# Moving all v loads to ScalarE's DMA queue, with a new search of every engine's order

**Chip, cores, metric.** One Trainium2 chip, one of its cores. The metric is device time in microseconds (us), the median of several executions.

## The reference

Attention in a window of 32 positions to both sides, for 8 batches of 8 heads of 576 x 64, then a gated linear recurrence over the sequence with two projections:

```python
scores = q @ k.T / sqrt(64);  mask = |i - j| <= 32;  attn = softmax(where(mask, scores, -1e9))
x = (attn @ v) as (batch, seq, 512)
val, gate = split(x @ w_in)                 # 512 -> 2 x 512
h[t] = exp(A_log)[0] * h[t-1] + val[t]
out = (gate * sigmoid(gate) * h) @ w_out    # 8 x 576 x 512, float32
```

## The kernel before

Five engines each work through a fixed order, held as a string with one letter per operation (`x` an exponential, `l` or `L` a load, `O` an output). Another string says which engine takes an operation that several could take. A search offline found both. Each engine runs its own list in order and waits, where it must, for the others. The loads of before are one list on SyncE:

```python
elif kd == "ld" and key[0] in "qk":            # 32 of them, 576 KB each, rows of 2304 bytes
    nc.sync.dma_start(out=..., in_=src[b].rearrange(...)[T])
elif kd == "ld" and key[0] == "v":             # 40 of them, rows of 256 bytes
    _, b, x = key
    lo = 128 * x - 32
    p0, p1 = max(0, -lo), min(128, S - lo)
    nc.sync.dma_start(out=bf("v32", b)[p0:p1, x],
                      in_=v[b, :, lo + p0:lo + p1, :].rearrange("h p d -> p h d"))
...
elif kd == "exp":                              # ScalarE alone, 36 of them, between scores and values
    nc.scalar.activation(bf("pr", *key), bf("sc", *key), AF.Exp, bias=0.0, scale=1.0 / 8.0)
...
elif kd == "mask":                             # where TensorE has not added the mask itself
    m = mask.rearrange("p r q -> p (r q)")
    pr = bf("pr", *key)
    (nc.vector if e == "dve" else nc.gpsimd).tensor_tensor(out=pr, in0=pr, in1=m[...], op=ALU.mult)
...
elif kd == "out":                              # 36 of them, 256 KB each
    nc.sync.dma_start(out=out_flat[r0:r0 + 128, :], in_=bf("o", *key))
...
idle = keep_busy(seq, place, 45.0)             # filler matmuls where TensorE is expected to wait
```

The issue of a transfer may first wait until an earlier transfer has landed. This waiting is done by the engine that issues.

The softmax here doesn't subtract the row's maximum and nothing guards it: scores larger than these inputs give would overflow.

Of the kernel before, what the change touches and what calls it, by code (L numbers as in the profile page):

```python
# [21 lines left out]
    ("pe", "xt"): (0.447, 0.66), ("pe", "pj"): (0.864, 1.07), ("pe", "fin"): (0.864, 1.07),  # L22
    ("act", "ev"): (1.012, 1.18), ("act", "exp"): (0.905, 1.09), ("act", "tanh"): (0.48, 0.63),
    ("act", "fev"): (0.495, 0.65), ("act", "cv"): (0.52, 0.68), ("act", "cw"): (0.52, 0.68),
# [11 lines left out]
ENGINES = ("pe", "act", "dve", "pool", "sp")  # L36
START = {"pe": 0.5, "act": 2.5, "dve": 0.5, "pool": 5.0, "sp": 0.8}
SWITCH, CAP, DLAT, DPRE = 0.095, 190, 1.75, 0.65
SLOTS = {"stg": 5, "q16": 2, "k16": 2, "qT": 3, "kT": 3, "v32": 2, "vE": 2, "vO": 2, "pr": 3,
         "rc": 2, "x16": 2, "xT": 2, "f2k": 16, "th": 3, "si": 3, "fu": 2}  # L40
LETTER = {"L": "ld", "w": "cw", "a": "ar", "k": "ck", "K": "trk", "E": "evk", "q": "cq", "Q": "trq",
          "e": "evq", "v": "cv", "h": "sh", "m": "mask", "S": "sc", "x": "exp", "P": "pv", "r":
          "rc", "n": "norm", "t": "xt", "T": "xe", "V": "pjv", "G": "pjg", "s": "scan", "g": "tanh",
          "u": "silu", "f": "fuse", "F": "fin", "o": "fev", "O": "out"}

SEQ = {
    "pe": "mQmQKSKKmSPSQPSmtmPSPSVtVGQGKGmSGPPmVStVPPGVKtGVVQGVSSFFFKGQFFQFmmSPSPKPPtSSFtKQVPPF"
          "GVSGtmmSVSPPVGSQtGKPPGVVSSGQKFVFSSPGFPPtGVQtKFGPSSGQKVFFGQVSSFtPPFVQtGKGPPSVGKVGVFFS"
          "SVGtFPPSFQtKVQVSSPGVGGFKFPPPFtVSSSGtFVGVGSPFFVFVPPPVFtGGVGVtGFVGGVFFFFFFF",
    "act": "qexExhxexwhwwxwwxgegEgxhvxTgkTEgwgegqxooxEgovooeoxxETxxEoeogxgTxxgxegEkvgvxxgeEooxxg"  # L50
           "kqogveEogxvxEgqooegxokxeogEgvxgvgEoxxogToxoeEexxgkgoEovgvoTxxgxoggooxoTggoTgogggoooo"
           "oo",
    "dve": "akaEehkhrnqrnETrnrnssTussuhvhurrnnshsrsrnnsussssusussvusmmqehvhurnrnrnrnqTmmrnrsnhhu"
           "ussrrnnsumTurrnnsushhmusrmmnrunrnTTusrnuhmeushsuTrnrnsTmurnusrunshshmsuurrnnmTssmrsu"
           "unrrnnrunhhsTusmsmrnuusmrnsrrnsunussssuusuussso",
    "pool": "aaqvkvvvvmwwwqkvvvfffqfwwwffkvvkffkvvvvvmqffkfqvvvfvqmfffkvfmvfqmffkkvfvvfmqfqmfvfvm"
            "fvfmffffffffff",
    "sp": "LLLLLLLLLLLLLLLLLLLLLLLLLLLLLLLLLLLLLLLLLLLLLLLLLLLLLLLLLLLLLLLLOLLOOLLLOLLLLLLLOOOL"
          "LLLOOLOLOLOOOLOOOOLOOOOOOOOOOOOOOOOOO",
}  # L60
SHARED = {
    "cw": "GAAAAAGGGGGA",
    "ar": "GDGD",
    "ck": "DGDGAGGGGAAGAGGA",
    "evk": "DADAAAAAAAAAAAAA",
    "cq": "AGDGGADDGGAGAGGG",
    "evq": "ADAAADAAAAADAAAA",
    "cv": "GGGGGGGDGADGAGDGGGGGGAAGGGAGAGGAAGGGAGAG",
    "sh": "DDAADDADDDDDDDDDDDDD",
    "mask": "pppGppppDDppDDGppDDDDGDGGDDGGDDGGDDD",  # L70
    "xe": "DDAAADADDDDDADADAA",
    "fev": "AAAAAAAAAAAAAAAAAAAAAAAAAAAAAAAAADAA",
}
ORDER = ["q01", "a", "q00", "k00", "v01", "v00", "w00", "k01", "k10", "v02", "v03", "q10",
         "v04", "w01", "w02", "w11", "w03", "w12", "w13", "w10", "q11", "k11", "v10", "v11",
         "v12", "v13", "v14", "k20", "q20", "v22", "w23", "w22", "w20", "w21", "v20", "q21",
         "k21", "v21", "q30", "v23", "v24", "k30", "k31", "q31", "v30", "v33", "v31", "v32",
         "v34", "v44", "q40", "k41", "k40", "v41", "q41", "v40", "v42", "v43", "q51", "q50",
         "v50", "v51", "k50", "k51", "v52", "v53", "v63", "q60", "v54", "v60", "k60", "q61",
         "v61", "k70", "v62", "k61", "v71", "v64", "q70", "q71", "v73", "v70", "v72", "k71",  # L80
         "v74"]
ORDER = [(x[0],) + tuple(int(y) for y in x[1:]) for x in ORDER]


def issue(o):
    return 0.9 if o.kind == "ld" and o.key[0] == "v" else 0.45


def DESC(o):

    return {"v": 48 if o.key[2:] in ((0,), (4,)) else 64, "q": 16, "k": 16, "w": 8, "a": 32}[o.key[0]] if o.kind == "ld" else 8

# [15 lines left out]
def build(order):  # L108
# [15 lines left out]
    g = last.get  # L124
    for it in order:
        if it[0] in "qk":
            add("ld", it, 0, ("sp",), 1.82, (), [("stg", it)])
        elif it[0] == "v":
            _, b, e = it
            add("ld", it, 0, ("sp",), 1.05 if e in (0, 4) else 1.3, (),  # L130
                [("v32", ("v32", b))])
        elif it[0] == "a":
            add("ld", it, 0, ("sp",), 0.8, ())
        else:
            add("ld", it, 0, ("sp",), 0.79, (), [("f2k", ("w32",) + it[1:])])
    for i in range(3):
        for a in range(4):
            add("cw", (i, a), 0.2 * i + 0.05 * a, ("dve", "act", "pool"), "cw", [g(("ld", "w", i, a))], (), [("w32", i, a)])
    for cc in range(4):
        add("ar", (cc,), 0, ("dve", "pool"), "ar", [g(("ld", "a"))])  # L140
    for b in range(B):
        for T in range(2):
            st = step_of(b, T)
            for n in "kq":
                c = add("c" + n, (b, T), st, ("pool", "dve", "act"), "cqk", [g(("ld", n, b, T))],
                        [(n + "16", (n + "16", b, T))], [(n, b, T)])
                t = add("tr" + n, (b, T), st, ("pe",), "tr", [c], [("ps2", ("tr" + n, b, T))], [(n + "16", b, T)])
                add("ev" + n, (b, T), st, ("act", "dve"), "ev", [t], [(n + "T", (n + "T", b))], [("tr" + n, b, T)])
        for e in range(5):
            add("cv", (b, e), step_of(b, 0) + 0.1 * e, ("pool", "act", "dve"), "cv", [g(("ld", "v", b, e))],  # L150
                [("vE", ("vE", b))], [("v32", b)])
        for T in (0, 1) if b < 2 else (2,):
            es = range(4) if T == 2 else range(2 * T, 2 * T + 2)
            for i in range(2):
                add("sh", (b, T, i), step_of(b, 0) + 0.1 * i, ("dve", "act"), "sh" if T == 2 else "sh1",
                    [g(("cv", b, e + i)) for e in es], [("vO", ("vO", b))], [("vE", b)])
# [22 lines left out]
    for c in range(NCH):  # L179
# [18 lines left out]
        for tt in range(4):  # L198
# [4 lines left out]
            e = add("fev", k, st, ("act", "dve") if c == NCH - 1 else ("act",), "fev", [f], [("f2k", ("o",) + k)], [("fo",) + k])  # L203
            add("out", k, st, ("sp",), 0.79, [e], (), [("o",) + k])
    return ops
# [4 lines left out]
def follow():  # L210
# [3 lines left out]
    kinds, users, place, held, used = {}, {}, {}, {}, {}  # L214
    eng_of = {"p": "pe", "A": "act", "D": "dve", "G": "pool"}
    for o in ops:
# [18 lines left out]
    tf = dict(START)  # L235
    mode, dma, lock, seq, ring = 0, 2.4, 0.0, [], []

# [3 lines left out]
    while len(seq) < len(ops):  # L241
# [26 lines left out]
        todo[e].pop()  # L268
        if e == "sp":
            dma = max(dma, s + issue(o) + DPRE) + o.cost  # L270
            o.end = dma + DLAT
            ring.append((dma, o.cost, DESC(o)))
            room, tf[e] = CAP, s + issue(o)
            for end, took, n in reversed(ring):
                if end <= tf[e]:
                    break
                if n > room:
                    tf[e] = max(tf[e], end - room / n * took)
                    break
                room -= n  # L280
# [68 lines left out]
def kernel(  # L349
# [39 lines left out]
    w_out16 = T([128, 4, 512], f16, "w_out16")  # L389

    for tl in bufs["v32"]:
        nc.vector.memset(tl[0:32, 0], 0.0)
        nc.vector.memset(tl[96:128, 4], 0.0)
# [45 lines left out]
    def emit(o):  # L439
# [11 lines left out]
        if kd == "ld" and key[0] in "qk":  # L451
# [4 lines left out]
                              in_=src[b].rearrange("(s y) (T p j) d -> T p s y (j d)", y=2, p=32, j=9)[T])  # L456
        elif kd == "ld" and key[0] == "v":
            _, b, x = key
            lo = 128 * x - 32
            p0, p1 = max(0, -lo), min(128, S - lo)  # L460
            nc.sync.dma_start(out=bf("v32", b)[p0:p1, x],
                              in_=v[b, :, lo + p0:lo + p1, :].rearrange("h p d -> p h d"))
        elif kd == "ld" and key[0] == "a":
            nc.sync.dma_start(out=a_log, in_=moe_A_log.rearrange("(a p) -> p a", p=128))
            nc.scalar.activation(a1, a_log, AF.Exp, bias=0.0, scale=1.0)
        elif kd == "ld":
# [141 lines left out]
        elif kd == "out":  # L608
            c, tt = key
            r0 = 512 * c + 128 * tt  # L610
            nc.sync.dma_start(out=out_flat[r0:r0 + 128, :], in_=bf("o", *key))

# [36 lines left out]
```

## Time and profile before

| | kernel before |
|---|---|
| time, median (range) of 3 runs | 175.58 us (174.99 to 175.94) |
| span of the profiled run (itself timed at 176.88 us) | 174.8 us |
| first real transposes, first output projection, last matmul's end | 11.17, 51.06, 171.2 us |

### The profile page before, as it was taken

Reading aid. Unit: us, or ns where it says so; the run is one execution under the profiler, and the core shown is the slowest. Engines: PE = TensorE matmul, PEld = TensorE weight load, DVE = VectorE, ACT = ScalarE, POOL = GpSimd, SP = SyncE. Lnnn points to the kernel's source line nnn. Section 1 sums busy time; section 2 is a strip of 40 time slices with the busy share of each in tenths; the row PEclk is TensorE's granted clock in tenths of the full one; section 3 lists DMA queues with packets and bytes.
Section 4 is the critical chain, followed back from the end, with each engine's and each line's share of the span. In section 5 each row is a group of like instructions: output and inputs, shape, how many; then the busy total and the mean of one; then the engine's idle time right before and its main releaser. Section 6 shows DMA issues by size and latency. Waiting matters only on the chain.

```text
span 174.8 us, 5309 instructions
## 1 busy us (share of the span) xinstructions
PE 162.5 (93%) x2178; PEld 101.8 (58%) x2178; DVE 144.6 (83%) x233; ACT 130.8 (75%) x172; POOL 114.9 (66%) x117
## 2 busy tenths in 40 slices
PE   1996999979999899999999999999999999999991
PEld 0343657848976585565647655654674654558740
DVE  5348467798999989999998899999979699899850
ACT  2232599886699998869999999877998993545552
POOL 7954409672699393499719879885999855505550
PEclk9999999999999999999999999999999999999999
DMA  4999999899999999999999999999950311401155
GB/s 125 293 294 271 313 373 288 162 326 325 329 208 344 226 219 342 270 245 267 264 307 267 325 303 348 262 323 311 353 174 4 120 64 60 161 23 60 64 212 208
DMA packets 53671, 41.23 MB, mean 236 GB/s; under 512 B 39312, under 2 KB 39312, under 8 KB 53648
## 3 DMA queue, kind: packets, MB, share of 16 engines
q1 hardware_dynamic: 53648, 40.90, 81.5%
q8 instruction: 17, 0.28, 0.7%
q14 instruction: 6, 0.05, 0.1%
HBM read 31.46 MB, written 9.44 MB: 234 GB/s over the span
## 4 chain that ended last, share of the span: by engine, by line
PE 65%; DVE 13%; ACT 8%; POOL 7%; issue 5%; POOLq 0%; ACTq 0%; DVEq 0%
PE psum L576 25%; PE psum L604 14%; PE psum L616 7%; PE psum L493 5%; PE psum L546 4%; PE psum L561 4%; PE psum L522 4%; DVE vO L425 3%; DVE si L589 3%; DVE f2k L584 2%; DVE pr L536 2%; ACT pr L527 2%; POOL fu L599 1%; ACT qT L422 1%; POOL pr L536 1%
## 5 line engine op out<-in xcount | busy, mean ns | idle before, releaser
L576 PE MATMUL psum<-xT,w_in 128*128 128x256 f16 (+1 forms) x384 | 69.9, 326 | 0.0
L576 PEld LDWEIGHTS <-w_in 128*128 128x128 f16 x384 | 35.5, 98 | 20.3 <-issue 0.2
L584 DVE TENSOR_TENSOR_SCAN f2k<-arep,f2k,psum 128x512 f32<-128x512 f32 (+1 forms) x44 | 44.4, 1029 | 1.9 <-PE psum L576 1.3
L527 ACT ACTIVATE pr<-psum 128x1024 f16<-128x1024 f32 x36 | 36.5, 1034 | 7.8 <-PE psum L522 7.4
L599 POOL TENSOR_TENSOR fu<-f2k,si 128x512 f16<-128x512 f32 x24 | 30.0, 1255 | 11.2 <-DVE si L589 7.0
L604 PE MATMUL psum<-w_out,fu 128*128 128x512 f16 x144 | 35.1, 379 | 0.1
L536 POOL TENSOR_TENSOR pr<-pr,mask 128x1024 f16<-128x1024 f16 x9 | 20.0, 2219 | 19.3 <-ACT pr L527 19.3
L587 ACT ACTIVATE th<-psum 128x512 f16<-128x512 f32 x36 | 21.8, 604 | 7.0 <-PE psum L576 6.9
L589 DVE SCALAR_TENSOR_TENSOR si<-th,psum 128x512 f16<-128x512 f16 x36 | 24.1, 676 | 3.0 <-ACT th L587 2.8
L422 ACT ACTIVATE f2k<-psum 128x512 f32<-128x512 f32 x35 | 20.8, 612 | 6.9 <-PE psum L604 6.2
L555 DVE TENSOR_TENSOR x<-psum,rc 128x512 f16<-128x512 f32 x36 | 24.1, 683 | 0.6
L596 POOL TENSOR_TENSOR fu<-f2k,si 128x512 f16<-128x512 f32 x12 | 14.8, 1232 | 13.7 <-DVE f2k L584 6.1
L429 POOL TENSOR_SCALAR vE<-v 128x512 f16<-128x512 f32 x27 | 18.2, 687 | 6.5 <-DMA v<-in_v_dram 6.5
L604 PEld LDWEIGHTS <-fu 128*128 128x128 f16 x144 | 13.2, 98 | 13.5 <-issue 0.2
L422 ACT ACTIVATE qT<-psum 128x1152 f16<-128x1152 f16 x13 | 14.8, 1141 | 3.9 <-PE psum L493 3.7
L422 ACT ACTIVATE kT<-psum 128x1152 f16<-128x1152 f16 x14 | 16.0, 1146 | 1.7 <-PE psum L493 1.7
L546 PEld LDWEIGHTS <-pr 128*64 128x64 f16 x576 | 11.4, 111 | 7.1 <-issue 4.5
L522 PEld LDWEIGHTS <-kT 64*128 64x128 f16 x576 | 10.4, 95 | 8.0 <-issue 4.5
L522 PE MATMUL psum<-qT,kT 64*128 64x64 f16 x576 | 13.5, 191 | 1.7 <-DVE kT L425 1.5
L546 PE MATMUL psum<-vO,pr 128*64 128x65 f16 x256 | 13.4, 197 | 1.7 <-DVE vO L425 1.7
L546 PE MATMUL psum<-vE,pr 128*64 128x65 f16 x320 | 14.0, 197 | 0.3 <-DVE pr L536 0.2
L616 PE MATMUL psum<-eye,ident 128*128 128x512 f16 x44 | 13.7, 457 | 0.4 <-ACT pr L527 0.4
(58 smaller groups left out, 198.7 us busy)
## 6 DMA issues: line engine op xcount, KB each, us to landing
stg<-in_q_dram SPq DMA_DIRECT2D x16, 576.0 KB, 7.2
stg<-in_k_dram SPq DMA_DIRECT2D x16, 576.0 KB, 6.6
out_dram<-f2k SPq DMA_DIRECT2D x36, 256.0 KB, 4.2
v<-in_v_dram SPq DMA_DIRECT2D x24, 256.0 KB, 7.4
v<-in_v_dram SPq DMA_DIRECT2D x16, 192.0 KB, 6.9
f2k<-in_moe_w_in_dram SPq DMA_DIRECT2D x8, 256.0 KB, 7.4
f2k<-in_moe_w_out_dram SPq DMA_DIRECT2D x4, 256.0 KB, 7.6
a_log<-in_moe_A_log_dram SPq DMA_DIRECT2D x1, 2.0 KB, 4.2
```

Source lines behind the costliest of these rows:

```text
L422: nc.scalar.activation(dst, src, AF.Copy, bias=0.0, scale=mul)
L522: nc.tensor.matmul(out=sc[:, h, 256 * t + 64 * r:256 * t + 64 * r + 64], lhsT=kT[64 * h:64 * h + 64, 64 * i:64 * i + 128], rhs=qT[64 * h:6 ...
L527: nc.scalar.activation(bf("pr", *key), bf("sc", *key), AF.Exp, bias=0.0, scale=1.0 / 8.0)
L536: (nc.vector if e == "dve" else nc.gpsimd).tensor_tensor(out=pr, in0=pr, in1=m[:, None, :].to_broadcast([128, 2, 512]), op=ALU.mult)
L546: nc.tensor.matmul(out=pv[p0:p0 + 64, h, x0:x0 + 65], lhsT=pr[:, h, at:at + 64], rhs=vt, start=True, stop=True)
L555: nc.vector.tensor_tensor(out=x, in0=view[:, :, :, 0:64], in1=bf("rc", *key)[:, :, :, None].to_broadcast([128, 2, 4, 64]), op=ALU.mult)
L576: nc.tensor.matmul(out=to, lhsT=w_in16[:, fc, 128 * w:128 * w + 128], rhs=xT[:, fc, t0:t0 + n], start=(fc == 0), stop=(fc == 3))
L584: nc.vector.tensor_tensor_scan(out=bf("h", c, x)[:, lo:lo + n], data0=arep[:, cc, a0:a0 + n], data1=bf("pjv", c, x)[:, lo:lo + n], initial ...
L589: nc.vector.scalar_tensor_tensor(out=bf("si", *key), in0=bf("th", *key), scalar=1.0, in1=bf("pjg", *key), op0=ALU.add, op1=ALU.mult)
L599: eng.tensor_tensor(out=bf("fu", c)[:, x, :], in0=bf("h", *key), in1=bf("si", *key), op=ALU.mult)
L604: nc.tensor.matmul(out=fo, lhsT=fu[:, cc, 128 * tt:128 * tt + 128], rhs=w_out16[:, cc, :], start=(cc == 0), stop=(cc == 3))
L616: nc.tensor.matmul(out=psum[:, bank, :], lhsT=ident, rhs=eye8.rearrange("p r q -> p (r q)"), start=True, stop=True)
```

## The change

Its intent: two queues instead of one. SyncE issues q, k and the weights; ScalarE issues v; the 36 outputs go to either (19 on SyncE, 17 on ScalarE). The search was run again with a model of two queues, so every order and assignment is new, as are a dummy exponential at the start and a separate place for the exponential of `A_log`. The core of the diff (order strings and model tables cut):

```diff
-        elif kd == "ld" and key[0] == "v":
-            _, b, x = key
+        elif kd == "lv":
+            b, x = key
...
-            nc.sync.dma_start(out=bf("v32", b)[p0:p1, x],
-                              in_=v[b, :, lo + p0:lo + p1, :].rearrange("h p d -> p h d"))
+            nc.scalar.dma_start(out=bf("v32", b)[p0:p1, x],
+                                in_=v[b, :, lo + p0:lo + p1, :].rearrange("h p d -> p h d"))
...
+        elif kd == "tb":
+            nc.scalar.activation(a1, a1, AF.Exp, bias=0.0, scale=1.0)
+        elif kd == "ae":
             nc.scalar.activation(a1, a_log, AF.Exp, bias=0.0, scale=1.0)
...
-            nc.sync.dma_start(out=out_flat[r0:r0 + 128, :], in_=bf("o", *key))
+            (nc.sync if e == "sp" else nc.scalar).dma_start(out=out_flat[r0:r0 + 128, :], in_=bf("o", *key))
...
 SEQ = {
-    "act": "qexexExhxexwhwwxwxgegEgxhvxTgkTEgwgegqxooxEgovooeoxxETxxEoeogxgTxxgxegEkvgvxxgeEooxxg" ...
+    "act": "lbllllvlAklkEvexlxllvvhxxeEwxxElewxwxglgTekgglEwkwggllolEolxvgooxxolllxgeEoxlxelEoxx" ...
```

## The prediction

> **What bounds the kernel now.** I read the busy shares first, then the slices, then the chain, then the waits, and last the order of each engine's work over time.
>
> ```profile
> PE 162.5 (93%) x2178; PEld 101.8 (58%) x2178; DVE 144.6 (83%) x233; ACT 130.8 (75%) x172; POOL 114.9 (66%) x117
> ...
> PE   1996999979999899999999999999999999999991
> ...
> DMA  4999999899999999999999999999950311401155
> ...
> q1 hardware_dynamic: 53648, 40.90, 81.5%
> ...
> PE 65%; DVE 13%; ACT 8%; POOL 7%; issue 5%; POOLq 0%; ACTq 0%; DVEq 0%
> ```
>
> TensorE (PE) is busy for 93% of 174.8 us and carries 65% of the chain that ended last. The DMA engines are full for the first three quarters, so it is tempting to call the loads the bound. The table of waits decides against it: between 40 and 96 us no engine waits for a load, and between 96 and 175 us none does either. Before 40 us they do. These are from the table of waits (waiting engine and tile, releaser, us in total, times, longest):
>
> ```profile
> POOL vE L429 <- DMA v<-in_v_dram: 6.5, 4, 2.2
> ACT a L465 <- DMA a_log<-in_moe_A_log_dram: 3.8, 1, 3.8
> DVE k L425 <- DMA stg<-in_k_dram: 2.6, 1, 2.6
> ```
>
> The busy share of PE also hides something. L616 is not work: it is 44 filler matmuls that keep the clock up while PE has nothing to do. PE's own timeline gives its places (start, us, count):
>
> ```profile
> 5.11 6.22 PE L616 MATMUL psum<-eye,ident 128*128 128x512 f16 x15
> 11.17 0.67 PE L493 MATMUL psum<-ident,q 128*128 128x128 f16 x9
> ...
> 15.58 2.33 PE L616 MATMUL psum<-eye,ident 128*128 128x512 f16 x10
> ...
> 51.06 2.76 PE L604 MATMUL psum<-w_out,fu 128*128 128x512 f16 x12
> ```
>
> So the first real work is at 11.17 us and the first output projection at 51.06. The last matmul ends at 171.2, and eviction and store take the last 3.6 us. To see where PE loses time I price its work by the steps that the chain shows when nothing holds them: nine transposes 0.50 us, 16 score matmuls 0.285 (0.57 for 32), 16 value matmuls 0.315 (0.63 for 32), eight transposes of x 0.45, four projection matmuls of width 512 0.86, an added mask pair 0.22 (from the timeline). By the built order there stand ahead of the first output projection 10 transpose groups, 10 scores, 8 value groups, 4 x-transposes, 15 projections, 7 masks: 5.0 + 2.9 + 2.5 + 1.8 + 12.9 + 1.5 = 26.6 us of work. It took 51.06 - 11.17 = 39.9 us. **Lost in the start: 13.3 us.** The whole order prices at 141.0 us, so 114.4 remain after 51.06; they took 171.2 - 51.06 = 120.1, with 5.7 us lost, much of it switches between matmul shapes. Hence: 11.2 head, 26.6 + 13.3 start, 114.4 + 5.7 steady, 3.6 tail. Only the head and the start have much to give. There ScalarE (ACT) is nearly full from 20 to 40 us (17.2 of 20 us), so the start is a chain of short supplies with ACT in it.
>
> **What the Trainium skill says.** "DMA: Bandwidth & Descriptors", section "Issuing engines are not separate DMA queues": issuing from several engines saves only sequencer time, the same 16 DMA engines do the work. The trace agrees as far as it can: the one queue already keeps the engines full, 98.9% in the first 45 us, at 278 GB/s. So the second queue by itself does not promise bandwidth. The same page, section "Queues, rings and completion order": each DMA engine goes round the queues that have work, packet by packet. No run of before can show that, with its one queue, but it matters here: v comes in 256-byte rows (most of the 39312 packets under 512 B), q and k in rows of 2304 bytes. If one packet of each is taken in turn, v gets about a tenth of the bytes while q or k is pending. "Perfetto Trace Analysis", section on the HWDGE DMA instruction: the recorded issue is not the transfer. The trace agrees: an issue of v took 608 ns at the median, its landing 7.2 us.
>
> **The change, part by part.**
>
> *SyncE* loses 40 v issues and 17 of the 36 outputs. Its long issues are stalls for room: the weight load issued at 5.01 us took 3.60 us, against about 0.4 for one that had room. But nothing waited for loads after 40 us, so this relief is worth something only in the start.
>
> *ACT* gains 57 issues. On SyncE a v issue cost 0.34 us at best and an output 0.33. If all of it were serial on ACT: 40 x 0.34 + 17 x 0.33 = 19 us. I take about half, since ACT's sequencer can issue while the previous activation runs (estimate): 10 us. Against that stands what the new order takes from ACT: 3 evictions of q/k (3 x 1.14), 4 of xT (4 x 1.02), 2 q conversions (2.3) and a weight conversion (0.6), less 5 v conversions (3.2) and a shift (1.07): -6.1 us. So ACT goes from 131 to about 135, still not the bound on average.
>
> *VectorE (DVE)*: three more evictions of q/k (3 x 1.35), four more xT (4 x 0.68), three products (3 x about 0.7), two weight conversions (0.9), less 6 masks (6 x 0.8), one q conversion (1.0), one v conversion (0.5) and one shift (0.7): about +3 us, to 147.5. *GpSimd* +4 masks (8.9), +3 q (3.6), -4 v (2.7), -3 products (3.7), -1 weight (0.6): about +5.5. *PE* +2 mask pairs, 0.45 us: 141.4.
>
> *The start.* The program now has 21 fillers ahead of the first transposes, not 15. At 0.41 us each from 5.1 us, the first transposes can't come before 13.7: **2.5 us later than now.** Behind them only 6 fillers are left (4 + 2), against 29. The author's order thus expects nearly no fillable gap after the start, where 29 fillers took 7.5 us. Ahead of the first output projection stand 24.2 us of work. Without any loss it would come at 13.7 + 24.2 = 37.9, not at 51.06. ACT can't follow that: ahead of and including the fourth tanh it has 8 exps (8.3), 7 evictions (8.0), 3 conversions of q/k (3.5), 4 of v (2.5), 3 of weights (1.9), 4 tanh (2.4), and 2.3 of the rest: 28.9 us, about 26 with the overlap of neighbouring activations that the timeline shows, and some 1.5 for six later issues. From a first k conversion at 11 to 15 us that is 38.5 to 42.5, against 43.2 now, before any wait. Allowing three or four us of waits, the first output projection comes at about 46.5. Then 117.2 us of work, 5.7 of steady losses and 3.4 of tail: 46.5 + 117.2 + 5.7 + 3.4 = **172.8 us of span**, 2.0 less than now. The timed median lies 0.8 above the span, so about 173.4.
>
> **Rivals.**
>
> *A: issue waits move onto ACT.* ACT runs in order, and a v issue with no room in its ring, or waiting for an earlier transfer, holds exps and evictions behind it. In the built order seven v issues stand ahead of the first k conversion and one more between it and the second; the very next one waits for an earlier DMA to land. With v starved by q/k packets, the first conversion could slip from 11 to 15 us and ACT could stall 3 or 4 us behind the first exp. Then most of the gain is gone: 176 to 178. For it: the 3.60 us stall seen above, landings of 7 us. Against it: SyncE stops by itself when its five staging buffers are full, which lets v through.
>
> *B: the order meets its plan.* The start loses only 5 us: 13.7 + 24.2 + 5 + 117.2 + 5.7 + 3.4 = 169.2. For it: the few fillers. Against it: the old order had fillers for 29 gaps and still lost 5.8 us beyond them (13.3 - 7.5).
>
> *C: the loads are hidden anyway, and VectorE binds.* Its work grows by 3 us and it already runs at 9.2 to 9.9 tenths from 40 to 130 us. What PE gains early would be given back there: 174 to 176. For it: DVE's 13% of the chain. Against it: PE starts its groups back to back there.
>
> **Range and chances.** The three rivals spread from 169 to 178. B would be faster by over 2% (below 172.1), the middle lies just inside 2%, and A at its worst comes near 179.1. Time 173.4, range 169.5 to 178: faster 0.33, same 0.55, slower 0.12.
>
> **What would show it.** First real transposes at 13.7 us or somewhat later; the first output projection between 44 and 49; no more than 6 fillers after the first transposes; DMA engines full until about 115 to 128 us; ACT's idle time with a DMA or nothing named as releaser below 5 us. It is wrong if ACT stands for many us at a v issue in the first 40 us (A), if the first output projection comes before 43 (B), or if it comes early and the 5.7 us of steady loss grow by as much (C).

## More of the kernel before

What ScalarE (ACT) waits for is the part that the change touches most. From the table of waits of the kernel before (engine, tile, line, releaser: us in total, times, longest), ACT alone:

```profile
ACT pr L527 <- PE psum L522: 7.4, 6, 2.7
ACT xT L422 <- PE psum L561: 7.0, 4, 3.4
...
ACT a L465 <- DMA a_log<-in_moe_A_log_dram: 3.8, 1, 3.8
...
ACT q L422 <- DMA stg<-in_q_dram: 1.9, 1, 1.9
...
ACT f2k L422 <- issue: 0.6, 1, 0.6
```

ACT waits for TensorE's results, the data it works on. A transfer delays it only twice, at the start.

## The result, and the profile after

| | before, same rounds | after |
|---|---|---|
| time, median (range) of 4 runs | 175.29 us (174.20 to 175.94) | **204.85 us** (203.38 to 205.41) |
| ratio, 95% interval | | 1.168 (1.159 to 1.177) |
| span of the profiled run | 174.8 us (an earlier run) | 202.7 us |

A ratio here and below is the mean time of one kernel's fast runs over the mean of the other's fast runs in the same rounds, so it is not quite the ratio of the medians quoted. The change makes the kernel slower by 17%, far outside the predicted range.

From the page of the kernel after: busy shares, 40 slices of 5.07 us in tenths (PEclk is the share of its full clock that TensorE was granted), queues, and the chain that ended last by engine.

```profile
PE 168.0 (83%) x2165; PEld 105.6 (52%) x2165; DVE 150.1 (74%) x237; ACT 130.2 (64%) x169; POOL 119.4 (59%) x116
...
PE   2964709999997089995599993999989999999992
...
PEclk9997885999999859999579999699999999999999
DMA  6999999914399984728935979949155511321155
...
q1 hardware_dynamic: 13696, 27.01, 39.1%
q10 hardware_dynamic: 39952, 13.90, 27.5%
...
PE 41%; DMA 19%; POOL 13%; DVE 8%; issue 6%; ACT 6%; ACTq 3%; SPq 1%; POOLq 0%; DVEq 0%
```

PE's row, solid before, now has holes. In the trace the gaps over 2 us run from 25.0 to 30.3, 64.7 to 71.6, 94.1 to 98.3 and 123.9 to 126.8 us, 19.4 us together. The DMA row, full to about 127 us before, drops to 1, 4 and 3 tenths at 40 to 56 us. In the chain, DMA has 19% and ACT's sequencer (ACTq) 3%, where the kernel before had no DMA at all and ACTq at 0%. ACT itself is no busier than before (130.2 against 130.8 us), so its work is not the cause. What it waits for is, from the table of waits, ACT alone:

```profile
ACT pr L528 <- DMA v<-in_v_dram: 8.1, 1, 8.1
ACT vE L420 <- issue: 7.7, 2, 5.3
...
ACT th L588 <- DMA out_dram<-f2k: 5.5, 1, 5.5
ACT vE L420 <- DMA a_log<-in_moe_A_log_dram: 4.9, 1, 4.9
...
ACT a L466 <- issue: 3.3, 1, 3.3
```

The first line is the telling one: `pr` is an exponential of scores. It has no use for v, and yet a v transfer is what ended its wait of 8.1 us. ACT's timeline shows why (start, us, operation, count, idle before and releaser; ACTq is the issue of a transfer):

```profile
60.02 1.93 ACT L528 ACTIVATE pr<-psum 128x1024 f16<-128x1024 f32 x2
61.83 0.62 ACT L420 ACTIVATE f2k<-psum 128x512 f32<-128x512 f32 x1
62.09 8.36 ACTq L459 DMA_DIRECT2D v<-in_v_dram  x3
70.55 1.02 ACT L528 ACTIVATE pr<-psum 128x1024 f16<-128x1024 f32 x1 [8.10 <-DMA v<-in_v_dram]
```

Three v issues stand ahead of that exponential and take from 62.09 to 70.45 us. The program as built has eight completion semaphores for its transfers and gives them out in turn, whichever queue issues. The trace of each issue gives the semaphore it uses, so one can look up when the transfer that used it before, the eighth back, landed (six of the issues):

```
v issue starts   its semaphore's earlier transfer   which landed at
     9.90                q or k (SyncE)                   9.88
    20.39                v      (ScalarE)                20.37
    22.48                weight (SyncE)                  22.46
    25.49                weight (SyncE)                  25.47
    67.79                v      (ScalarE)                67.72
    96.31                k      (SyncE)                  96.29
```

The issues start within 0.08 us of a landing that has nothing to do with them except the semaphore. I count two kinds of hold over all 57 issues on ACT. One is from when the sequencer came free to that landing: 24.7 us in sum. The other is what an issue takes beyond 0.40 us, the usual duration with room in the queue: 12.4 us (the longest issue took 2.77). I call the second kind a wait for room; it is not a wait for SyncE's own issues, since beside five of the eight issues over 1 us SyncE issued nothing. Together **ACT is held for 37.1 us** by issues. This is the sequencer's time: about 5 us of the first kind lie under an activation that was still running. The four long gaps of PE each go with such holds (issues between 22 and 27, 62 and 70, 92 and 96, 122 and 125 us).

The chain of the kernel after, in order of time (start, us, what), passes through such a hold:

```profile
90.96 5.33 DMA stg<-in_k_dram
96.31 0.35 ACTq L459
...
97.27 1.02 ACT pr L528
98.33 0.61 PE psum L523 x16
```

A k transfer lands, ACT can issue its v load, only then does it run an exponential, and TensorE's next scores wait for that one.

Why do transfers land so late? Here are the two queues in the stretch 56 to 68 us of the kernel after (packets, MB, share of the 16 engines' time; then what was issued there, KB, median us to landing):

```profile
q1 hardware_dynamic: 1525, 3.27, 76.8%
q10 hardware_dynamic: 2465, 0.62, 24.4%
v<-in_v_dram ACTq DMA_DIRECT2D x3, 256.0 KB, 11.7
```

v (q10) gets 62% of the packets, 16% of the bytes and about a quarter of the time: its packets are small. A v load of 256 KB takes 11.7 us to land. In the same stretch of the kernel before it took 7.6:

```profile
v<-in_v_dram SPq DMA_DIRECT2D x3, 256.0 KB, 7.6
```

q and k come in such a burst because SyncE stood still before it. SyncE's timeline:

```profile
34.37 0.61 SPq L453 DMA_DIRECT2D stg<-in_q_dram  x1
54.87 0.35 SPq L612 DMA_DIRECT2D out_dram<-f2k  x1
55.31 0.61 SPq L453 DMA_DIRECT2D stg<-in_q_dram  x1
```

The first output stands in SyncE's list ahead of 20 of its 45 loads, and its data are late (ACT starts that eviction at 54.24), since the start was late. The loads behind it wait 20 us. That is the hole in the DMA row at 40 to 56 us; then all come at once and starve v.

### The profile page after: what moved, and what is told of

It reads as the page before. It is cut to its first block, busy times and chain, and to the rows that moved or that the text cites. A ratio compares the mean times of both kernels' runs of the same rounds, so it can differ in the third digit from the quotient of the medians.

```text
span 202.7 us, 5267 instructions
## 1 busy us (share of the span) xinstructions
PE 168.0 (83%) x2165; PEld 105.6 (52%) x2165; DVE 150.1 (74%) x237; ACT 130.2 (64%) x169; POOL 119.4 (59%) x116
## 4 chain that ended last, share of the span: by engine, by line
PE 41%; DMA 19%; POOL 13%; DVE 8%; issue 6%; ACT 6%; ACTq 3%; SPq 1%; POOLq 0%; DVEq 0%
PE psum L577 16%; PE psum L605 10%; DMA stg<-in_k_dram 9%; DMA stg<-in_q_dram 7%; PE psum L494 5%; DMA f2k<-in_moe_w_in_dram 4%; DVE f2k L585 3%; POOL pr L537 3%; PE psum L562 3%; PE psum L547 3%; POOL fu L597 3%; POOL q L427 3%; PE psum L523 3%; ACTq L459 2%; ACT pr L528 2%
## 5 line engine op out<-in xcount | busy, mean ns | idle before, releaser
L577 PE MATMUL psum<-xT,w_in 128*128 128x256 f16 (+1 forms) x384 | 72.0, 330 | 0.2 <-DVE xT L423 0.2
L528 ACT ACTIVATE pr<-psum 128x1024 f16<-128x1024 f32 x36 | 35.5, 1024 | 13.1 <-DMA v<-in_v_dram 8.1
L605 PE MATMUL psum<-w_out,fu 128*128 128x512 f16 x144 | 38.2, 399 | 1.2 <-DVE si L590 1.1
L537 POOL TENSOR_TENSOR pr<-pr,mask 128x1024 f16<-128x1024 f16 x13 | 29.6, 2285 | 14.5 <-ACT pr L528 14.4
L600 POOL TENSOR_TENSOR fu<-f2k,si 128x512 f16<-128x512 f32 x24 | 28.0, 1177 | 14.2 <-DVE si L590 9.4
L420 ACT ACTIVATE f2k<-psum 128x512 f32<-128x512 f32 x35 | 21.0, 599 | 12.7 <-PE psum L605 11.2
L597 POOL TENSOR_TENSOR fu<-f2k,si 128x512 f16<-128x512 f32 x9 | 10.4, 1160 | 23.6 <-DVE si L590 19.6
L427 POOL TENSOR_SCALAR q<-stg 128x1152 f16<-128x1152 f32 x12 | 15.1, 1265 | 6.4 <-DMA stg<-in_q_dram 3.1
L420 ACT ACTIVATE kT<-psum 128x1152 f16<-128x1152 f16 x13 | 14.7, 1127 | 6.3 <-PE psum L494 6.3
L420 ACT ACTIVATE vE<-v 128x512 f16<-128x512 f32 x15 | 9.2, 628 | 14.6 <-issue 7.7
L494 PE MATMUL psum<-ident,q 128*128 128x128 f16 x144 | 12.1, 236 | 7.0 <-ACT pr L528 7.0
L547 PEld LDWEIGHTS <-pr 128*64 128x64 f16 x576 | 11.8, 115 | 11.4 <-ACT pr L528 5.4
L427 POOL TENSOR_SCALAR vE<-v 128x512 f16<-128x512 f32 x23 | 15.8, 694 | 3.3 <-DMA v<-in_v_dram 3.3
```

Of the source, the lines that this page charges most:

```text
L420: nc.scalar.activation(dst, src, AF.Copy, bias=0.0, scale=mul)
L427: nc.gpsimd.tensor_scalar(out=dst, in0=src, scalar1=mul, scalar2=1.0, op0=ALU.mult, op1=ALU.mult)
L547: nc.tensor.matmul(out=pv[p0:p0 + 64, h, x0:x0 + 65], lhsT=pr[:, h, at:at + 64], rhs=vt, start=True, stop=True)
L577: nc.tensor.matmul(out=to, lhsT=w_in16[:, fc, 128 * w:128 * w + 128], rhs=xT[:, fc, t0:t0 + n], start=(fc == 0), stop=(fc == 3))
L600: eng.tensor_tensor(out=bf("fu", c)[:, x, :], in0=bf("h", *key), in1=bf("si", *key), op=ALU.mult)
L605: nc.tensor.matmul(out=fo, lhsT=fu[:, cc, 128 * tt:128 * tt + 128], rhs=w_out16[:, cc, :], start=(cc == 0), stop=(cc == 3))
```

## Experiments

**Theory 1**: v issues on ScalarE hold exponentials and evictions, because ScalarE runs in order and these issues wait. **Rivals**: outputs ahead of loads on SyncE (2); v's small packets alone (3); the new orders are worse (4). The expectations of runs 1 to 4 call this last one theory 3; in those of runs 5, 6 and 9, theory A is the packets and theory B the waits. All experiments have 3 rounds. A time is the median of all executions; in runs 3 to 7, 13 and 14 one or two of them are slow. Differences called fast means use fast executions alone.

**1. The changed kernel with v issued from SyncE again.** Edit: `nc.scalar.dma_start` to `nc.sync.dma_start` at the v load, nothing else.

> The changed kernel with its v loads issued from SyncE again, at the same places of the program; orders of the compute engines, buffers and the split of the outputs stay. Theory 1 (ScalarE held by v issues that wait for room or for an earlier transfer): ScalarE is free of these waits, so most of the 29 us come back, 173 to 182 us. Theory 2 (SyncE held by outputs that stand ahead of loads): nothing of that is undone and v now stands behind these outputs too, so 200 us or more. Theory 3 (the new compute orders are slow by themselves): about 200 us.

Measured: 177.09 us (176.06 to 178.49), ratio to before 1.008 (1.000 to 1.016). This one word removes 27.8 us of 204.85. So the new orders as such are not the loss; v on ScalarE's queue is. TensorE's timeline shows the plan met at first:

```profile
43.26 1.03 PE L605 MATMUL psum<-w_out,fu 128*128 128x512 f16 x4
```

The first output projection comes 7.8 us earlier than before (51.06). Yet the end is no earlier; that is taken up with runs 10 to 14.

**2. All outputs on ScalarE, v there too; 3. all outputs on ScalarE, v on SyncE.**

```diff
-            (nc.sync if e == "sp" else nc.scalar).dma_start(out=out_flat[...], in_=bf("o", *key))
+            nc.scalar.dma_start(out=out_flat[...], in_=bf("o", *key))
```

> The changed kernel with all 36 outputs on ScalarE's queue, so that none stands ahead of a load on SyncE; v loads stay on ScalarE. Theory 1: ScalarE's v issues still wait, 195 to 207 us. Theory 2: the 20 us hole without q and k loads from 35 to 55 us is gone and most of the loss with it, 176 to 188 us. Theory 3: about 204 us.

> The changed kernel with v loads on SyncE and all outputs on ScalarE: both suspects are undone. Theories 1 and 2: 171 to 179 us, as the plan of the new orders had it. Theory 3: 195 us or more.

Measured: 200.96 us (ratio 1.144, 1.137 to 1.151) and 180.83 us (1.027, 1.020 to 1.034). Moving the outputs away from SyncE's loads gains little, some 4 us of the 29.6, net of what they cost on ScalarE. There they hold it too: 9.1 + 2.3 us by the count above, 3.3 us of time over run 1 (fast means), so that run 3 missed the expected 171 to 179.

**4. The kernel before with v issued from ScalarE**, all its orders kept.

> The kernel before with only its v loads moved to ScalarE's queue, at the same places of the program; old orders, outputs on SyncE, the first of them late. Theory 1: ScalarE now waits in its v issues, 185 to 210 us. Theory 2: the outputs stand where they stood, so no loss, 173 to 178 us. Theory 3: the old orders are good, 173 to 178 us.

Measured: 194.05 us, ratio 1.098 (1.086 to 1.110). The orders of before suffer too (ACT held for 14.3 + 9.7 us), so the loss belongs to the queue, not to one order.

**5. The changed kernel with v in contiguous rows of 2048 bytes, on ScalarE** (wrong: the same bytes into the same places, but not the same values).

```diff
-            nc.scalar.dma_start(out=bf("v32", b)[p0:p1, x],
-                                in_=v[b, :, lo + p0:lo + p1, :].rearrange("h p d -> p h d"))
+            flat = v[b].rearrange("h p d -> (h p d)").rearrange("(r c) -> r c", c=512)
+            nc.scalar.dma_start(out=bf("v32", b)[p0:p1, x].rearrange("p h d -> p (h d)"),
+                                in_=flat[lo + p0:lo + p1, :])
```

> The changed kernel, v still loaded from ScalarE, but each tile as 2048-byte rows in memory order (a wrong result on purpose: the bytes of v land in other places, their number and all instructions stay). A v load is then 8 packets per DMA engine and not 64. Theory A (the cause is the packets: the two queues take turns packet by packet, so v with its 256-byte packets lands late and fills its queue): ScalarE's waits at its issues fall from 37 us (25 for an earlier transfer, 12 for room) to under 10 us, time 172 to 184 us. Theory B (the cause is the order alone: ScalarE must wait for the eighth transfer before, which is often a q or k load that SyncE issued late): only the 12 us for room go, the rest stays, 192 to 200 us.

Measured: 188.69 us, ratio 1.069 (1.060 to 1.079; the profiled run was slow). It lies between the ranges of the two theories, so both missed. Waiting for room fell from 12.4 to 2.8 us, the waits for earlier transfers only from 24.7 to 23.0. So packets matter (3), but what remains is 1.

**6. q and k on ScalarE, v and weights on SyncE.** Edit: the two `dma_start` lines exchange their engines.

> The changed kernel with the roles exchanged: q and k loads from ScalarE, v, weights and 19 outputs from SyncE. q and k are 16 packets per load[...]. Theory A: ScalarE has little to wait for, 174 to 186 us. Theory B: any load on ScalarE that waits for a staging buffer or an earlier transfer holds it, 190 us or more.

Measured: 210.76 us, ratio 1.195 (1.185 to 1.205). q and k have large packets and are only 32 issues, and yet ACT is held longer: 40.4 us for earlier transfers and 8.3 for room, for which theory A had left no place. It is not something about v. The waits of ACT in this kernel:

```profile
ACT vE L420 <- DMA stg<-in_q_dram: 17.1, 2, 9.8
...
ACT vE L420 <- DMA f2k<-in_moe_w_in_dram: 6.1, 1, 6.1
```

With v or with q and k, the loads that ran ahead on an engine that also computes stopped the computing.

**7. Only v(0,0) to v(0,2) on ScalarE, in the changed kernel; 8. the same three, issued first, in the kernel before.** Only the earliest issues are moved, when eight transfers are not yet out.

```diff
-            nc.scalar.dma_start(out=bf("v32", b)[p0:p1, x],
+            (nc.scalar if (b, x) in ((0, 0), (0, 1), (0, 2)) else nc.sync).dma_start(out=bf("v32", b)[p0:p1, x],
```

> The changed kernel with only the first three v loads on ScalarE (they waited for nothing in the trace), the other 37 on SyncE. Both theories: ScalarE doesn't wait, q and k come a little earlier at the start; 175 to 178 us, about as with all v on SyncE (177.1).

> The kernel before with only the first three v loads on ScalarE, ahead of everything else there; old orders. A search for a version that beats both: the start has two queues and nothing waits in ScalarE. 173.5 to 176.5 us against 175.6; a gain of 1 to 2 us if q, k and the first weights land earlier.

Measured: 176.68 us (ratio 1.001, 0.993 to 1.010) and 175.87 us (1.000, 0.994 to 1.005). Harmless, and of no measurable use: no version tried that computes the right result is faster than the kernel before.

**9. The changed kernel with ScalarE's v issues (from the fourth on) up to 8 instructions later in its order.** Edit: the letters `l` in ScalarE's string move right, nothing else.

> The changed kernel with the fourth and every later v issue standing up to 8 instructions further back in ScalarE's order, never behind its own consumer there; nothing else in the orders changes. Theory B (ScalarE is held at an issue until the eighth transfer before has landed): later issues find it landed more often, ScalarE's 25 us of waits for transfers fall by a third or more, 188 to 198 us. Theory A (packets, a full queue): the same bytes meet the same turns and v comes later still, 200 us or more.

Measured: 228.52 us, ratio 1.300 (1.295 to 1.305): a clear miss of theory B's range; it lies where theory A had it. The waits of ACT's issues for earlier transfers did fall, from 24.7 to 3.5 us, as theory B said; but now v itself is late, as theory A said. The two largest waits of this kernel:

```profile
POOL vE L427 <- DMA v<-in_v_dram: 51.3, 7, 14.9
ACT vE L420 <- DMA v<-in_v_dram: 32.6, 8, 12.0
```

The place of an issue on an engine that computes is a squeeze. Early, the issue holds the engine; late, the data are late. SyncE, which has nothing else to do, can stand at an issue early at no cost.

**10. The rows of run 5, with v on SyncE; 11. the rows in the kernel before**. Their outputs are wrong, which doesn't matter for the times.

> The changed kernel with v on SyncE and in 2048-byte rows (wrong result on purpose). Beside e5 it differs only in the engine that issues v, beside e1 (177.1 us) only in v's packets. If the early lead of the new orders (first output projection at 43.3 us in e1) is given back because the one queue brings q and k too slowly, cheaper v packets give it back to us: 168 to 173 us. If it is given back to VectorE's or GpSimd's work, 174.5 to 177. The difference e5 - e10 is then the cost of ScalarE's waits for transfers alone: 12 to 20 us expected.

> The kernel before with v in 2048-byte rows on SyncE (wrong result on purpose). Nothing waited for loads after 40 us, so cheaper loads can only help the start: 173 to 175.5 us against 175.6. If the loads did bind after all: below 171.

Measured: 177.32 us (ratio 1.006, 0.999 to 1.012) and 175.49 us (0.998, 0.994 to 1.001). Cheaper v loads are worth nothing when SyncE issues them, so the loads bind neither order. Run 10 lies just above both of its ranges and is level with run 1. It also splits the loss. Runs 5 and 10 differ in the issuing engine alone, both with large packets: 188.1 - 177.2 = 10.9 us (fast means; 12 to 20 were expected). I put this down to ACT's waits for earlier transfers, since waits for room are nearly gone in run 5. Small packets on ScalarE (room, starved landings) add 204.6 - 188.1 = 16.5 us; on SyncE they add nothing. That the two sum to the loss of run 1 only says that runs 1 and 10 are equal. These runs are not all of the same rounds, but the medians of before beside them lie within 0.7 us.

**12 to 14. Where does run 1's early lead go?** The new order with v on SyncE is 7.8 us ahead at the first output projection and level at the end. Rival C of the prediction says that VectorE (DVE) gives it back. Run 12 leaves out the 10 mask products on VectorE in the kernel of run 1; run 13 the 13 on GpSimd instead; run 14 the 16 on VectorE in the kernel before. Their outputs are wrong, which doesn't matter for the times.

```diff
-            (nc.vector if e == "dve" else nc.gpsimd).tensor_tensor(out=pr, in0=pr, in1=m[...], op=ALU.mult)
+            if e == "dve":
+                return
+            nc.gpsimd.tensor_tensor(out=pr, in0=pr, in1=m[...], op=ALU.mult)
```

> The kernel of the first run (changed order, v issued from SyncE) without its ten mask products on VectorE (9.3 us of VectorE's work; wrong results on purpose: 10 of 36 groups are not masked). If VectorE binds between 43 and 130 us and gives the early lead back there (rival C), a large part of the 9.3 us shows: 169 to 173 us. If the order or another engine binds there, 175.5 to 177.5.

> The kernel of the first run without its 13 mask products on GpSimd (some 29 us of GpSimd's work at 2.2 us each; wrong results on purpose), VectorE's kept. If VectorE binds, 175 to 177, since it keeps all its work. If the long GpSimd masks between exponential and value matmuls are what gives the lead back, 168 to 173.

> The kernel before without its 16 mask products on VectorE (some 13 us of its work; wrong results on purpose). A control: TensorE is busy for 98 to 100% of 40 to 140 us there, so both theories expect little: 173 to 175.5 us. If this kernel gains as much as the first of these three runs, VectorE's load is no explanation of the difference between the two orders.

Measured: 174.74 us (ratio 0.996, 0.991 to 1.001), 175.49 us (0.996, 0.991 to 1.002) and 174.23 us (0.989, 0.982 to 0.995; the profiled run was slow and is not used). Run 12 missed the 169 to 173 of rival C and lies below the other range too. Run 13 lies in the 175 to 177 that was written down for VectorE as the bound. But run 14, the control, gains as much as run 12, which by its text speaks against VectorE: taking work from VectorE or from GpSimd (0.996 for both, against run 1's 1.008), and from VectorE in the kernel before (0.989), each give a little over 1%. VectorE is not shown to be the bound. Windows of 20 us of run 1 and of run 13 say more (the first number after the window's length is PE's busy time; then PEld, DVE, ACT, POOL, granted clock, DMA share, GB/s). Run 1:

```profile
40.00:60.00 20.00, 19.48 (x312) 14.19 (x311) 18.24 (x31) 17.45 (x24) 15.37 (x19) 1.00 1.06 294
60.00:80.00 20.00, 18.06 (x269) 11.16 (x267) 19.03 (x24) 15.62 (x19) 14.85 (x16) 1.00 1.00 278
80.00:100.00 20.00, 19.73 (x282) 11.39 (x281) 19.20 (x29) 16.82 (x23) 18.52 (x15) 1.00 1.07 271
100.00:120.00 20.00, 18.14 (x232) 10.67 (x225) 19.59 (x22) 16.74 (x22) 16.40 (x14) 1.00 0.97 303
120.00:140.00 20.00, 19.10 (x285) 11.31 (x284) 18.30 (x30) 15.40 (x23) 14.02 (x10) 1.00 0.41 120
```

PE is idle for 5.5 us of these 100. The same five windows leave 1.1 us in the kernel before, 2.8 in run 12 and 1.3 in run 13. Without GpSimd's masks most of this idle time is gone, without VectorE's half. Leaving a mask out also shortens the way from an exponential to its value matmuls, so the runs do not tell an engine's load from the length of that way. PE of run 13 (PE's busy time, granted clock, DMA share, GB/s):

```profile
40.00:60.00 20.00, 20.00 (x320) 1.00 1.08 301
60.00:80.00 20.00, 19.95 (x281) 1.00 1.04 290
80.00:100.00 20.00, 20.00 (x302) 1.00 1.09 285
```

Even with PE this full, the span is only 172.3 us, so lighter engines beside PE bring little more from this order. The account from the first output projection to the last matmul's end is 128.9 us in run 1 (43.26 to 172.20) and 120.1 before, 8.8 more. Of these, 2.8 were never a lead: the new order puts that much more of its priced work behind the first output projection (117.2 against 114.4). Another 4.4 are idle PE. The remaining 1.6 fit dearer busy time: PE's real matmuls take 151.0 us in run 1 and 148.8 before (busy time less fillers, 159.7 - 8.7 and 162.5 - 13.7), partly from two more mask pairs.

## Why the prediction was wrong

| term, us | before | predicted | after | run 1 |
|---|---|---|---|---|
| head, to the first transposes | 11.2 | 13.7 | 12.95 | 12.5 |
| start: work + lost | 26.6 + 13.3 | 24.2 + 8.6 | 24.2 + 16.0 | 24.2 + 6.6 |
| from the first output projection: work + lost | 114.4 + 5.7 | 117.2 + 5.7 | 117.2 + 28.4 | 117.2 + 11.7 |
| tail | 3.6 | 3.4 | 3.9 | 3.9 |
| span | 174.8 | 172.8 | 202.7 | 176.1 |

- **The step that failed** is "Allowing three or four us of waits", with the same size in rival A ("ACT could stall 3 or 4 us behind the first exp"; "176 to 178"). The mechanism was named rightly: ACT runs in order, a v issue waits for room or for an earlier transfer, exponentials and evictions stand behind it. The term was mis-sized: it measured 37.1 us of held ACT, about 17 of them ahead of the first output projection, where 3 or 4 were allowed, and about 20 after it, where none were. I looked for it in the first 40 us only and priced the rest with the old 5.7. It recurred at 62, 92, 117 and 121 us: 28.4 were lost after the first output projection, against 11.7 in run 1.
- **"SyncE stops by itself when its five staging buffers are full, which lets v through"** did not hold enough. SyncE stopped for 20 us, but behind an output, when v did not need the room, and then sent a burst. v landed in 11.7 us in that stretch. The starving itself was foreseen; v got 16% of the bytes there, where I had worked out a tenth. That tenth took a row for a packet; the page's packet is several descriptors, so the nearness is partly luck.
- **"I take about half ... 10 us"** of serial issue cost was too much in the other direction. A v issue with room takes 0.33 to 0.39 us on ACT and can lie inside a running activation: the one at 36.68 to 37.01 us lies inside an exponential that runs from 36.18 to 37.20. The cost of an issue is not its duration but what it waits for.
- **Work moved between engines** was right in sign. DVE rose by 5.5 us to 150.1, not by 3 to 147.5. ACT's activations, summed over its groups, fall from 143.3 to 138.0 us, so by 5.3 against 6.1 predicted. Its busy time, in which overlapping neighbours count once, falls by 0.6 us only, since fewer of them follow each other closely.
- **Head and fillers**: 12.95 instead of 13.7, since the 21 fillers took 5.86 us and not 21 x 0.41 = 8.6. They ended at 11.4, and the transposes then waited 1.5 us for ACT's conversion of k, so the near hit has another cause than the one given. Six fillers stood after the first transposes, as read from the order.
- **DMA full until 115 to 128 us** and **ACT idle below 5 us for DMA or nothing**: both wrong, and by the tests stated there they pointed to A.
- **Rival B** was right about the start once v is on SyncE: 6.6 us lost (it said 5), first output projection at 43.26 (it implied 42.9). **Rival C**'s size (174 to 176) nearly fits run 1's span of 176.1, but its cause holds only in part: the steady loss grew by 6.0 us, and VectorE is not alone in it.
- **A second-order loss I had not priced**: PE's clock. PE's real matmuls take 160.1 us after (168.0 - 7.9 of fillers), against 151.0 in run 1 with the same instructions. The mean granted clock was 0.932 and 0.995, and in 20 to 40 us of the kernel after 0.79. In the trace after, each of the four long gaps of PE is followed, 2.6 to 4.7 us after it began, by a stretch of 3.4 or 6.8 us at half the clock (a fifth such stretch, from 18.2 us, follows shorter gaps); run 1, with no gap over 2 us after its first matmuls, has none before its end. No run here changes the one without the other. Of the 26.6 us between the two spans, idle PE is 18.3 (34.7 against 16.4) and busy PE 8.3 (168.0 against 159.7).
- **Small misreadings.** Six v issues, not seven, stand ahead of the first k conversion (ACT's string `lbllllvlAk`). VectorE's busy tenths in 40 to 130 us are 8.9 to 9.9, not 9.2 to 9.9. The "0.8" between median and span takes them from different executions: the profiled one took 176.88 us. None of them bears on the step that failed.

What stays open: how much of the 16.5 us of small packets is room in the queue and how much is late landing. Nor did a run change the number of completion semaphores; that they are what ACT's issues wait for rests on the waits recorded with the issues and on the coincidences of times. And VectorE's and GpSimd's shares in run 1's idle PE are not separated: without its masks GpSimd's load falls, but VectorE's busy time falls too, from 150.0 to 145.4 us, with the same instructions.

## What to carry to other kernels

Before moving transfers to a second queue, ask what its issuing engine does when an issue has to wait: on an engine that computes in order, every wait for room or for an earlier transfer becomes a wait of the work behind it, whatever that work needs. Keep a stream of loads that runs ahead on an engine with nothing else to do, and read a "free" issue slot by what the transfers around it will be doing, not by the 0.4 us the issue takes. When a wait's releaser is a transfer that the waiting instruction does not use, look at the issues that stand ahead of it.

## What the Trainium skill lacked or had wrong

- "DMA: Bandwidth & Descriptors", section "Issuing engines are not separate DMA queues", says that issuing from several engines "will only save the time on the sequencer". On bandwidth the runs agree: in 20 to 40 us, with nearly the same mix of packets, the kernel after moved 352 GB/s over two queues and run 1 moved 342 over one. That the issuing sequencer does the waiting, and is free for its next instruction only after the issue, is in "Perfetto Trace Analysis" (HWDGE DMA instruction). What both lack is the cost of that on an engine that computes: the work behind a waiting issue stands, here 37.1 us on ScalarE and, with the packet effects, 27.8 us of time.
- The same page, section "Queues, rings and completion order", says that each engine takes the queues in turn, packet by packet. The shares fit that, though no run shows the turns of one engine: a queue of 256-byte rows beside one of 2304-byte rows had 62% of the packets, 16% of the bytes, and landings of 11.7 us instead of 7.6. The page does not give this consequence.
- "Perfetto Trace Analysis", on the HWDGE DMA instruction, says that the recorded issue is not the transfer. True here, and as it says a wait for a semaphore stands outside the recorded issue: it shows as a gap ahead of it, up to 5.25 us. What it lacks: a recorded issue can be long while small packets are queued (2.77 us, against 0.33 to 0.39 otherwise). I read this as a wait for room; in run 5, with an eighth of v's packets, this excess fell from 12.4 to 2.8 us.
- "Perfetto Trace Analysis", on the DVE and Act instruction, says that the sequencer is ready for its next instruction once the activation is pushed. It gives no example with a DMA issue; here one lies inside a running activation at no visible cost (0.33 us inside a 1.02 us exponential).
